# Output stores moved to ScalarE's DMA queue, and the U and V loads moved behind the last chunk of batch 0

## The chip, the core and the metric

The kernel runs on one core of one Trainium2 chip. The time is device microseconds (us) of one execution. The core has five engines that run side by side and wait for each other on semaphores: TensorE (PE in the profile, PEld for its weight loads), VectorE (DVE), ScalarE (ACT), GpSimd (POOL) and SyncE (SP). SyncE only starts DMAs here. In the traces below, VectorE, ScalarE and SyncE take their instructions in program order: a small copy on VectorE stands behind an addition that waits 18.8 us, although its own input is long ready. The granted clock is TensorE's clock as the chip granted it, as a share of full speed (1.00).

## The reference, cut to what matters

```python
# q, k, v: (4 batches, 8 heads, 768 positions, 64); out: (4, 768, 512), float32
for t in range(S):                                   # retention, per head
    state = gamma * state + outer(k[t], v[t])
    y[t] = scale * q[t] @ state
x = y as (B, 768, 512)
h = x.transpose(0, 2, 1) @ U @ V                     # U: 768x32, V: 32x768
u = x + h.transpose(0, 2, 1)
out = u + relu(u @ w_ch1) @ w_ch2                    # 512 -> 2048 -> 512
```

The kernel does the retention in 6 chunks of 128 positions per batch. It weaves the chunk work of batch b into the MLP of batch b-1.

## The kernel before

All inputs come through one list of loads, `feed`. SyncE issues the loads in that order into a ring of 28 buffers of 128x512 float32, and so runs up to 28 buffers ahead of GpSimd, which scales the inputs or casts them to bfloat16. U and V stand behind chunk 3 of batch 0 in the list.

```python
outp = ctx.enter_context(tc.tile_pool(name="outp", bufs=3))   # three output buffers
...
def feed_one():                         # the next load, on SyncE
    ...
    if key[0] == "uv":
        nc.sync.dma_start(out=Uf, in_=moe_U.rearrange("(j p) r -> p j r", p=P))
        for c in range(NCB):
            nc.sync.dma_start(out=Vf[ds(RK * c, RK)], in_=moe_V)
        return
    ...
    nc.sync.dma_start(out=t, in_=src)
...
for ci in range(NCK):
    feed_chunk(0, ci)
    if ci == 3:
        feed.append((("uv",), None))
# then w1 (16 tiles), batch 1's chunk 0, w2 (16 tiles), batch 1's chunk 1, ...
```

The last piece of each block of 128 output rows adds `u` and stores the result. The store is on SyncE too, behind every load that the program has issued up to then:

```python
def down(j, m0):                        # 4 of the 16 matmuls of output block j
    def f():
        ...
        if m0 == NM - 4:
            o_sb = outp.tile([P, DM], fp32, tag="o_sb", ...)
            nc.vector.tensor_tensor(o_sb, ch, us[b][:, j], op=ALU.add)
            nc.sync.dma_start(out=out[b, ts(j, P)], in_=o_sb)
    return f

def weave(pieces, *tracks):             # MLP pieces, other steps put between them
    ...
    for cost, f in pieces:
        while marks and marks[0][0] <= at:
            marks.pop(0)[1]()
        f()
        at += cost
...
weave(mlp_pieces(b - 1), (first, 0.03, 0.3),
      (steps, 0.42 if b == 1 else 0.15, 0.97))   # steps: chunks of batch b, then low rank
```

## Time and profile before

The time before is 270.7 us (median of 4 runs, 270.19 to 270.91). The profiled execution has a span of 267.2 us.

| stretch (us) | what TensorE does | PE busy | granted clock |
|---|---|---|---|
| 0 to 34.8 | batch 0's chunks, waiting for loads | 19.0 | 0.87 |
| 34.8 to 88.4 | batch 0's MLP, batch 1's chunks woven in | 50.9 of 53.6 | 0.96 (0.89 up to 56.7 us, then 1.00) |
| 88.4 to 102.9 | nothing | 0.2 of 14.5 | 0.58 |
| 102.9 to 111.7 | rest of the same stage | 8.2 of 8.8 | 0.72 |
| 111.7 to 220.8 | batches 1 and 2 | 107.4 of 109.1 | 1.00 |
| 220.8 to 267.2 | batch 3 | 42.4 of 46.4 | 1.00 |

From the page of the kernel before, the span in 40 slices of 6.7 us, counted from 1: busy tenths of TensorE, its granted clock in tenths, busy tenths of the DMA engines.

```profile
PE   1774689988999205999999999999999999999994
PEclk9996759999999755999999999999999999999999
DMA  8999998999999999697001021100001111000212
```

DMA is nearly full up to slice 19. TensorE is full from slice 7, but for a hole in slices 14 and 15, and the clock is low behind the hole. The waits view of the kernel before (engine, line, what was waited for, us, times, longest) names the two waits of the hole:

```profile
DVE o_3_1327 L335 <- DMA out_dram<-o_0_1089: 18.8, 1, 18.8
PE s_1372 L280 <- DVE pc_1366 L73: 14.3, 1, 14.3
```

Its timeline (start, us, engine, line, operation, output<-input, idle before and what ended it) gives the order of events on VectorE, SyncE and TensorE:

```profile
69.97 0.69 DVE L335 TENSOR_TENSOR o_0_1089<-mlp_1018,u_588 128x512 f32<-128x512 f32 x1 [2.32 <-PE mlp_1018 L330]
...
87.55 1.04 PE L330 MATMUL mlp_1332<-w2b,gT_685 128*128 128x512 bf16 x4
...
96.32 1.06 SPq L108 DMA_DIRECT2D in_1066<-in_q_dram  x1
97.47 1.07 SPq L336 DMA_DIRECT2D out_dram<-o_0_1089  x1
...
101.98 0.69 DVE L335 TENSOR_TENSOR o_3_1327<-mlp_1268,u_588 128x512 f32<-128x512 f32 x1 [18.83 <-DMA out_dram<-o_0_1089]
102.59 0.28 DVE L73 CAST pc_1366<-o_1341 128x128 bf16<-128x128 f32 x1
...
102.92 0.26 PE L280 MATMUL s_1372<-pc_1366,V_85 32*128 32x128 bf16 x1 [14.34 <-DVE pc_1366 L73]
...
111.69 1.03 PE L307 MATMUL mlp_1444<-uT_1331,w1b 128*128 128x512 bf16 x4
```

The addition o_0 was done at 70.66 us. SyncE issued its store at 97.47, 26.8 us later, behind further loads of about 1.1 us each. The fourth output block, o_3, needs o_0's buffer, so VectorE stood. The small copy of pc stands behind o_3 on VectorE, and TensorE needs pc. What the loads do to TensorE earlier shows at batch 1's chunk 1, again from the timeline of before:

```profile
57.24 1.04 POOL L174 TENSOR_TENSOR qd_1_916<-in_543,gq 128x512 bf16<-128x512 f32 x1 [0.67 <-DMA in_543<-in_q_dram]
58.52 0.38 PE L207 MATMUL qk_928<-ident,qd_1_916 128*128 128x128 bf16 x4
59.47 0.40 PE L209 MATMUL qk_928<-ident,kd_1_920 128*128 128x128 bf16 x4 [0.57 <-POOL kd_1_920 L174]
60.93 0.38 PE L217 MATMUL st_897<-vd_1_924,kd_1_920 128*128 128x128 bf16 x4 [1.06 <-POOL vd_1_924 L172]
```

GpSimd takes the chunk up as the loads land, and TensorE waits for GpSimd. At this point TensorE runs at the pace of the loads.

### The profile page before, as it was taken

What the parts mean: (1) busy time and instruction counts of PE and PEld (TensorE: products, weight loads), DVE (VectorE), ACT (ScalarE), POOL (GpSimd) and SP (SyncE); (2) the same over time, 40 slices, a digit from 0 to 9 for tenths busy, and PEclk for the clock granted to TensorE, in tenths of its full rate; (3) what the DMA queues carried; (4) which work ended last, traced back from release to release, by engine and by line L of the source; (5) the groups of instructions that cost most, each with busy time, mean ns of one, the idle gap of its engine ahead of it and who ended that gap; (6) DMA issues with size and microseconds to landing.
All of it is one profiled execution on the core that took longest, in us unless ns stands there. A gap on an engine that the chain in (4) does not pass through costs nothing.

```text
span 267.2 us, 4715 instructions
## 1 busy us (share of the span) xinstructions
PE 228.2 (85%) x1898; PEld 131.3 (49%) x1924; DVE 97.1 (36%) x178; ACT 95.1 (36%) x179; POOL 85.5 (32%) x113
## 2 busy tenths in 40 slices
PE   1774689988999205999999999999999999999994
PEld 1453524475555102445685545467855454475441
DVE  3330434523443004245554343455543425222211
ACT  2562334467442000346650203466611033552000
POOL 4766777877576700002333710030000000000000
PEclk9996759999999755999999999999999999999999
DMA  8999998999999999697001021100001111000212
GB/s 165 218 213 209 312 353 245 383 244 219 201 223 208 223 224 257 165 224 124 2 2 39 39 82 39 42 0 2 0 19 63 67 53 40 2 0 0 81 79 79
DMA packets 83942, 34.36 MB, mean 129 GB/s; under 512 B 76624, under 2 KB 76624, under 8 KB 83920
## 3 DMA queue, kind: packets, MB, share of 16 engines
q1 hardware_dynamic: 83920, 34.05, 55.0%
q8 instruction: 15, 0.25, 0.4%
q14 instruction: 7, 0.06, 0.1%
HBM read 27.75 MB, written 6.29 MB: 127 GB/s over the span
## 4 chain that ended last, share of the span: by engine, by line
PE 65%; DMA 19%; SPq 9%; POOL 2%; issue 2%; ACT 1%; DVE 1%; POOLq 0%; DVEq 0%
SPq L108 8%; DMA in_261<-in_q_dram 2%; DMA in_147<-in_moe_w_ch_dram 2%; DMA in_445<-in_moe_w_ch_dram 2%; DMA in_674<-in_q_dram 2%; DMA in_552<-in_q_dram 2%; DMA in_131<-in_moe_w_ch_dram 2%; DMA in_540<-in_moe_w_ch_dram 2%; DMA in_922<-in_v_dram 2%; DMA out_dram<-o_0_1089 2%; PE mlp_2807 L330 1%; PE mlp_2097 L330 1%; PE mlp_1183 L330 1%; PE mlp_2636 L330 1%; PE mlp_1988 L330 1%
## 5 line engine op out<-in xcount | busy, mean ns | idle before, releaser
L307 PEld LDWEIGHTS <-w1b 128*128 128x128 bf16 x512 | 48.2, 99 | 32.4 <-issue 3.0
L330 PEld LDWEIGHTS <-gT_2879 128*128 128x128 bf16 x96 | 9.4, 98 | 11.1
L280 PEld LDWEIGHTS <-V_85 32*128 32x128 bf16 x96 | 3.0, 98 | 21.9 <-issue 21.9
L330 PEld LDWEIGHTS <-gT_2169 128*128 128x128 bf16 x96 | 8.5, 98 | 8.9
L330 PEld LDWEIGHTS <-gT_1443 128*128 128x128 bf16 x96 | 8.5, 98 | 8.9
L280 PE MATMUL s_1372<-pc_1366,V_85 32*128 32x128 bf16 x4 | 0.6, 297 | 14.3 <-DVE pc_1366 L73 14.3
L330 PEld LDWEIGHTS <-gT_685 128*128 128x128 bf16 x96 | 8.4, 100 | 8.3 <-issue 1.5
L174 POOL TENSOR_TENSOR qd_5_1902<-in_926,gq 128x512 bf16<-128x512 f32 x1 | 1.0, 1042 | 25.9 <-PE qk_1520 L207 25.9
L71 ACT ACTIVATE uT_1331<-qk_1408 128x1024 bf16<-128x1024 bf16 x1 | 1.0, 1024 | 23.2 <-PE qk_1408 L292 23.2
L335 DVE TENSOR_TENSOR o_3_1327<-mlp_1268,u_588 128x512 f32<-128x512 f32 x1 | 0.7, 692 | 18.8 <-DMA out_dram<-o_0_1089 18.8
L174 POOL TENSOR_TENSOR qd_5_2612<-in_1554,gq 128x512 bf16<-128x512 f32 x1 | 1.0, 1042 | 19.9 <-PE qk_2240 L207 19.9
L207 PE MATMUL qk_194<-ident,qd_0_182 128*128 128x128 bf16 x4 | 0.6, 308 | 5.0 <-POOL qd_0_182 L174 5.0
L330 PE MATMUL mlp_1332<-w2b,gT_685 128*128 128x512 bf16 x15 | 4.8, 446 | 0.1
L330 PE MATMUL mlp_1403<-w2b,gT_685 128*128 128x512 bf16 x15 | 4.4, 430 | 0.3 <-issue 0.3
L330 PE MATMUL mlp_1183<-w2b,gT_685 128*128 128x512 bf16 x15 | 4.1, 381 | 0.1
L330 PE MATMUL mlp_1018<-w2b,gT_685 128*128 128x512 bf16 x15 | 4.1, 380 | 0.1
L330 PE MATMUL mlp_2636<-w2b,gT_2169 128*128 128x512 bf16 x15 | 3.9, 380 | 0.1
L330 PE MATMUL mlp_1875<-w2b,gT_1443 128*128 128x512 bf16 x15 | 3.9, 380 | 0.1
L330 PE MATMUL mlp_1926<-w2b,gT_1443 128*128 128x512 bf16 x15 | 3.9, 380 | 0.1
L330 PE MATMUL mlp_1268<-w2b,gT_685 128*128 128x512 bf16 x15 | 3.9, 380 | 0.1
L330 PE MATMUL mlp_2585<-w2b,gT_2169 128*128 128x512 bf16 x15 | 3.9, 380 | 0.1
L71 ACT ACTIVATE uT_2042<-qk_2129 128x1024 bf16<-128x1024 bf16 x1 | 1.0, 1023 | 8.2 <-PE qk_2129 L292 8.2
(980 smaller groups left out, 591.8 us busy)
## 6 DMA issues: line engine op xcount, KB each, us to landing
Vf<-in_moe_V_dram SPq DMA_DIRECT2D x4, 96.0 KB, 3.5
in_90<-in_q_dram SPq DMA_DIRECT2D x1, 256.0 KB, 3.0
in_92<-in_k_dram SPq DMA_DIRECT2D x1, 256.0 KB, 3.7
in_94<-in_v_dram SPq DMA_DIRECT2D x1, 256.0 KB, 4.3
in_96<-in_q_dram SPq DMA_DIRECT2D x1, 256.0 KB, 4.8
in_98<-in_k_dram SPq DMA_DIRECT2D x1, 256.0 KB, 5.0
in_100<-in_v_dram SPq DMA_DIRECT2D x1, 256.0 KB, 5.1
in_102<-in_q_dram SPq DMA_DIRECT2D x1, 256.0 KB, 5.1
```

The costliest lines, as they stand in the source:

```text
L71: nc.scalar.activation(dst, src, AF.Copy)
L108: nc.sync.dma_start(out=t, in_=src)
L174: nc.gpsimd.tensor_tensor(t, src, g[:, ci, :, None].to_broadcast([P, H, D]), op=ALU.mult)
L207: nc.tensor.transpose(tp[:, ts(p, P)], qd[:, ds(2 * p, 2)], ident)
L280: nc.tensor.matmul(banks[c - c0][:, ts(j - j0, P)], V4[ds(RK * c, RK), ts(j, P)], pcs[b][ds(RK * c, RK)], start=True, stop=True)
L307: nc.tensor.matmul(g_p[:, :sz], w1b[:, c, ts(m, P)], uTs[b][:, c, ds(lo, sz)], start=(c == 0), stop=(c == NCB - 1))
L330: nc.tensor.matmul(ch, gT[:, m, ts(j, P)], w2b[:, m], start=(m == 0), stop=(m == NM - 1))
L335: nc.vector.tensor_tensor(o_sb, ch, us[b][:, j], op=ALU.add)
```

## The change

There are two intents. Stores should not stand behind loads, so they go on ScalarE's queue, one MLP piece later, so that ScalarE does not wait for the addition. And batch 0's chunks 4 and 5 should not wait for U and V, which are needed only after chunk 5.

```diff
     for ci in range(NCK):
         feed_chunk(0, ci)
-        if ci == 3:
-            feed.append((("uv",), None))
+    feed.append((("uv",), None))
...
+    stores = []
+
+    def store():
+        if stores:
+            dst, src = stores.pop(0)
+            nc.scalar.dma_start(out=dst, in_=src)
...
-                    nc.sync.dma_start(out=out[b, ts(j, P)], in_=o_sb)
+                    stores.append((out[b, ts(j, P)], o_sb))
...
+            late = len(stores)
             f()
+            if late:
+                store()
             at += cost
         for _, f in marks:
             f()
+        while stores:
+            store()
...
             prep_chunk(0, ci + 1)
-            if ci + 1 == 3:
-                prep_uv()
+        else:
+            prep_uv()
```

## The prediction

> **What bounds the kernel now.** The slice view shows the DMA engines at 9 tenths for the first 97 us and TensorE at 9 tenths after 103. Between them is a hole. Timeline: the addition o_3 of batch 0 on VectorE waits 18.8 us (83.2 to 102.0) for the store of o_0, as there are three output buffers. That store was ready at 70.7, but SyncE reached it only at 97.5, behind some 25 input loads of about 1.1 us each (timeline of DMA issues). The copy of pc queues behind o_3, and TensorE idles from 88.4 to 102.9: 14.3 us in the waits view. The granted clock is then 0.50 to about 107.9 (2 us windows): four 128x512 matmuls take 1.82 us in place of 0.86.
>
> **The stores' move.** On ScalarE's queue the o_0 store issues near 71 us and lands about 4.4 later (its latency before), long before o_3 wants the buffer. The hole goes. From 88.4 to 111.7 TensorE took 23.3 us; the work in it at full clock is about 5.8 (24 matmuls of 0.216, 16 small expansions, 16 transposes), plus 0.5 of waits for the one transpose bank: 6.3. Gain about 17.0 us.
>
> Cost: 24 issues of 0.38 (free queue) to 1.1 us (full queue) on ScalarE, which is 36% busy and idles 0.7 to 2 us between instructions there; at most 0.3 us on the critical path. The Trainium skill ("DMA: Bandwidth & Descriptors", "Issuing engines are not separate DMA queues") says both queues share the 16 engines: six stores (1.5 MB) delay batch 2's loads by some 4 to 7 us at 220 to 380 GB/s. TensorE wants those only after 100 us; GpSimd had prepared most by 94. No loss. In batches 1 and 2, SyncE's waits of 23 and 32 us never held TensorE: each takes 54.5 us with TensorE busy 53.7.
>
> **The move of U and V.** Chunks 4 and 5 are prepared about 3.5 us earlier (U and V take 13.13 to 16.60 of SyncE's issue). The first MLP piece starts near 32 in place of 34.8, held by the first w1 casts (four done at 31.8). But the total of loads is the same and DMA is saturated: batch 1's chunk 1 still comes at 58.4 to 61, where TensorE already waits 1.9 us. The 3 us are paid back there. Worse, a gap near 3 us may drop the clock: the Trainium skill ("TensorE: Matmul & The Clock Gate", "Part 1: The HAM clock gate") says an idle window of about 3.4 us throttles to half; this trace agrees (the 2.84 us gap at 20 us and the 14.3 us one both led to 0.50, for about 5 us after work resumed). Between 0.5 us gained and 2.5 lost; I take 0.6 lost.
>
> **Prediction.** 270.66 - 17.0 + 0.6 = 254.3 us, range 251.8 to 257.0. Faster by over 2% 0.97, within 2% 0.025, slower 0.005.
>
> **What would show it.** Right: no wait of o_3 for the store; the 14.3 us wait for pc gone, clock 1.00 from 66 us on; stores on a second queue, landing in 3 to 6 us; the first MLP matmul near 32, but larger waits for batch 1's chunk 1 at 55 to 61; batches 1 and 2 still 54.5 us each, last batch 46.4. Wrong on U/V: that chunk arriving before 57.
>
> **What would make it wrong.** Stores starved by the loads' backlog, so that o_3 still waits; ScalarE's issue blocking so long that x and state evictions hold TensorE; stores slowing batch 1's chunk 5, which has 2.4 us of slack; a clock drop near 58 costing more than 2.5.

## The result

The changed kernel took 255.44 us (median of 4 runs, 254.50 to 256.59) against 270.7. The ratio is 0.9441, 95% interval 0.9391 to 0.9490, so it is faster, inside the predicted range of 251.8 to 257.0. A ratio here is the mean time of one kernel's fast runs over that of the other's of the same rounds, so it is not quite the ratio of the medians.

The same three rows from the page after (span 254.4 us, so slices of 6.4 us):

```profile
PE   0785789973999989999999999999999999999993
PEclk9997779996799999999999999999999999999999
DMA  8999899998999999999401111000012110000122
```

The hole at slices 14 and 15 is gone. There is a new, smaller one at slice 10, with a low clock behind it. Timeline after, at the old hole:

```profile
72.99 0.69 DVE L342 TENSOR_TENSOR o_0_1089<-mlp_1018,u_588 128x512 f32<-128x512 f32 x1 [2.31 <-PE mlp_1018 L337]
73.72 0.37 ACTq L303 DMA_DIRECT2D out_dram<-o_0_1089  x1
...
88.50 0.69 DVE L342 TENSOR_TENSOR o_3_1327<-mlp_1267,u_588 128x512 f32<-128x512 f32 x1 [2.33 <-PE mlp_1267 L337]
90.57 1.04 PE L337 MATMUL mlp_1331<-w2b,gT_685 128*128 128x512 bf16 x4
91.54 0.23 PE L279 MATMUL s_1372<-pc_1366,V_85 32*128 32x128 bf16 x1
...
98.92 1.03 PE L314 MATMUL mlp_1444<-uT_1330,w1b 128*128 128x512 bf16 x4
```

The o_0 store goes out 0.04 us after its addition ends (72.99 + 0.69) and lands 3.7 us later (list of DMA issues). The addition o_3 now waits for TensorE only, and TensorE meets pc without a wait. From the end of the four matmuls before pc is used to the next batch's first up-projection, TensorE took 23.3 us before (88.4 to 111.7) and 7.5 now (91.4 to 98.9): 15.8 us less. (The end of four matmuls is taken as 0.86 us after their start, since the next can start before the listed 1.04 us are over.)

At batch 1's chunk 1 the timeline after reads:

```profile
59.78 1.04 POOL L173 TENSOR_TENSOR qd_1_916<-in_543,gq 128x512 bf16<-128x512 f32 x1 [0.49 <-DMA in_543<-in_q_dram]
60.88 0.61 PE L206 MATMUL qk_928<-ident,qd_1_916 128*128 128x128 bf16 x4 [5.21 <-POOL qd_1_916 L173]
62.03 0.61 PE L208 MATMUL qk_928<-ident,kd_1_920 128*128 128x128 bf16 x4 [0.54 <-POOL kd_1_920 L173]
```

TensorE's MLP started at 32.7 us in place of 34.8, and TensorE reached this point about 3 us earlier than before. But the chunk came 2.5 us later than before. The gap of 5.2 us let the clock fall, as the 2 us windows after show (window, length, busy us of PE, PEld, DVE, ACT, POOL, granted clock, DMA share, GB/s):

```profile
58.00:60.00 2.00, 0.00 (x0) 0.00 (x0) 0.00 (x0) 0.00 (x0) 1.43 (x4) 0.95 0.52 114
60.00:62.00 2.00, 0.61 (x4) 0.35 (x4) 0.00 (x0) 0.00 (x0) 1.87 (x2) 0.50 0.93 207
62.00:64.00 2.00, 1.90 (x13) 1.47 (x14) 0.00 (x0) 1.26 (x2) 1.43 (x2) 0.50 1.01 214
```

So two questions were open. Is the whole gain the stores', and what about the late stores had cost the time? And does the U/V move bring anything, or does it cost, and through what?

### The profile page after: what moved, and what is told of

Its sections match the earlier page's. It is cut to its first block, busy times and chain, and to the rows that moved or that the text cites. A ratio compares the mean times of both kernels' runs of the same rounds, so it can differ in the third digit from the quotient of the medians.

```text
span 254.4 us, 4715 instructions
## 1 busy us (share of the span) xinstructions
PE 227.9 (90%) x1898; PEld 132.5 (52%) x1924; DVE 97.1 (38%) x178; ACT 95.0 (37%) x179; POOL 85.4 (34%) x113
## 4 chain that ended last, share of the span: by engine, by line
PE 71%; DMA 12%; SPq 10%; issue 2%; DVE 1%; ACT 1%; POOL 1%; POOLq 0%; DVEq 0%
SPq L108 9%; DMA in_543<-in_q_dram 3%; DMA in_257<-in_moe_w_ch_dram 3%; DMA in_145<-in_moe_w_ch_dram 3%; DMA in_491<-in_moe_w_ch_dram 2%; DMA in_321<-in_moe_w_ch_dram 2%; PE mlp_2096 L337 1%; PE mlp_2806 L337 1%; PE mlp_1182 L337 1%; PE mlp_2585 L337 1%; PE mlp_2697 L337 1%; PE mlp_1987 L337 1%; PE mlp_1925 L337 1%; PE mlp_2635 L337 1%; PE mlp_1018 L337 1%
## 5 line engine op out<-in xcount | busy, mean ns | idle before, releaser
L206 PE MATMUL qk_194<-ident,qd_0_182 128*128 128x128 bf16 x4 | 0.6, 305 | 5.3 <-POOL qd_0_182 L173 5.3
L206 PE MATMUL qk_928<-ident,qd_1_916 128*128 128x128 bf16 x4 | 0.6, 309 | 5.2 <-POOL qd_1_916 L173 5.2
L237 DVE TENSOR_TENSOR a_1_0_967<-s_957,mask 128x512 bf16<-128x512 f32 x1 | 0.7, 692 | 9.4 <-PE s_958 L233 9.4
L337 PE MATMUL mlp_1182<-w2b,gT_685 128*128 128x512 bf16 x15 | 4.1, 381 | 0.1
L337 PE MATMUL mlp_1018<-w2b,gT_685 128*128 128x512 bf16 x15 | 4.1, 380 | 0.1
L337 PE MATMUL mlp_1331<-w2b,gT_685 128*128 128x512 bf16 x15 | 3.9, 381 | 0.1
L337 PE MATMUL mlp_2585<-w2b,gT_2169 128*128 128x512 bf16 x15 | 3.9, 380 | 0.1
L337 PE MATMUL mlp_2635<-w2b,gT_2169 128*128 128x512 bf16 x15 | 3.9, 380 | 0.1
L337 PE MATMUL mlp_1925<-w2b,gT_1443 128*128 128x512 bf16 x15 | 3.9, 380 | 0.1
L337 PE MATMUL mlp_1267<-w2b,gT_685 128*128 128x512 bf16 x15 | 3.9, 380 | 0.1
L337 PE MATMUL mlp_1875<-w2b,gT_1443 128*128 128x512 bf16 x15 | 3.9, 380 | 0.1
L337 PE MATMUL mlp_1105<-w2b,gT_685 128*128 128x512 bf16 x15 | 3.7, 380 | 0.2 <-issue 0.2
```

Of the source, the lines that this page charges most:

```text
L206: nc.tensor.transpose(tp[:, ts(p, P)], qd[:, ds(2 * p, 2)], ident)
L237: nc.vector.tensor_tensor(a, four(sp[i]), causal(mask), op=ALU.mult)
L337: nc.tensor.matmul(ch, gT[:, m, ts(j, P)], w2b[:, m], start=(m == 0), stop=(m == NM - 1))
```

## The experiments

Theory A says: the gain comes from taking away VectorE's wait for a store; the U/V move costs time, as TensorE only arrives earlier at loads that come no earlier. Rivals are named with each run. "Changed kernel" means the kernel after. Each ratio is against the kernel before in the same rounds; the intervals are 95%. All twelve runs computed the right result.

### The changed kernel again, on the chip of the next three

No edit.

> The changed kernel once more, to have it on the chip of the three runs beside it and to see its two groups of times (254.5 to 254.7 at a granted clock of 0.98, 256.2 to 256.6 at 0.966). Expected 254 to 257 us. Theory A (the gap before batch 1's chunk 1 sometimes costs the full clock and sometimes not): slow and fast times of this kernel again differ by the clock, about 2 us for 0.013 of clock. Rival: the times scatter at one clock.

Measured: 255.08 us median of 5 (254.25 to 255.14), ratio 0.9449 (0.9423 to 0.9476). The part on the clock failed: a run at a mean clock of 0.965 took 255.14 us, one at 0.980 took 255.08. Mean granted clock and time do not go together here.

### The stores' move alone

```diff
-    feed.append((("uv",), None))          # and prep_uv behind chunk 5
+        if ci == 3:
+            feed.append((("uv",), None))  # and prep_uv behind chunk 3, as before
```

> The stores' move alone; U and V stay behind chunk 3. Theory A (the whole gain is the stores', and the U/V move costs time, because it only makes TensorE arrive earlier at batch 1's chunk 1, whose loads come no earlier): 252 to 254 us, 1 to 3 us below the changed kernel; before chunk 1 TensorE waits 1.9 us in three waits as before, and the clock stays 1.00 from 42 us on. Rival B (the U/V move brings its 3 us and the stores' move less than 17): 256 to 258.5 us, above the changed kernel.

Measured: 253.44 us median of 4 (253.09 to 253.84), ratio 0.9396 (0.9370 to 0.9422). The mean is 253.46 against 254.92 of the changed kernel on the same chip, and no run of the one reaches a run of the other. The stores' move gains 16.3 us (269.76 - 253.46), and the U/V move on top costs 1.5. The clock is 1.00 from 42 us on and the waits before chunk 1 are the old ones, 0.34 and 0.97 us. Rival B falls.

### The U/V move alone

```diff
-        if ci == 3:
-            feed.append((("uv",), None))
+    feed.append((("uv",), None))          # prep_uv behind chunk 5; stores on SyncE
```

> The U/V move alone; stores stay on SyncE as before. Theory A: 270 to 273 us, no faster than before: a gap of 3 to 5 us before batch 1's chunk 1, and the hole at o_3 still ends when SyncE reaches the o_0 store at about 97.5 us or up to 2 us later. Rival B: about 267.5 us.

Measured: 269.77 us median of 6 (269.25 to 271.62), ratio 1.0009 (0.9979 to 1.0039). The gap before chunk 1 is 4.3 us. The old hole stays, 14.0 us of waiting for pc, and swallows the loss: it ends when SyncE reaches the o_0 store, at 98.07 us. The move brings nothing alone.

### Six output buffers, nothing else

```diff
-    outp = ctx.enter_context(tc.tile_pool(name="outp", bufs=3))
+    outp = ctx.enter_context(tc.tile_pool(name="outp", bufs=6))
```

> The kernel before with six output buffers in place of three, and nothing else: the stores stay on SyncE behind the loads, U and V stay. It tells what about the late store cost the time. Theory A (only the wait of o_3, o_4, o_5 for a buffer stops VectorE, then TensorE): the hole goes although the o_0 store still goes out near 97 us; 252 to 254.5 us, like the stores' move alone. Rival C (the stores on SyncE's queue cost time also by holding back the loads, or the second queue is needed for bandwidth): the time stays above 257 us.

Measured: 253.67 us median of 5 (253.13 to 254.23), ratio 0.9403 (0.9378 to 0.9428): the same as the stores' move alone. Its timeline shows that the o_0 store is as late as ever and o_3 no longer cares:

```profile
85.89 0.69 DVE L335 TENSOR_TENSOR o<-mlp,u 128x512 f32<-128x512 f32 x1 [2.33 <-PE mlp L330]
...
97.96 1.90 SPq L336 DMA_DIRECT2D out_dram<-o  x1
```

So the late store itself cost nothing, nor did SyncE's queue need relief. The whole cost was the reuse of the buffer. A second queue and three more buffers (6 KB in each partition) are two cures of one wait. Rival C falls.

### Stores later, but still on SyncE

```diff
-            nc.scalar.dma_start(out=dst, in_=src)     # in the stores' move alone
+            nc.sync.dma_start(out=dst, in_=src)
```

> The kernel before with the stores one MLP piece later but still on SyncE's queue. Theory A: nothing is gained, 269 to 271 us; the o_0 store still goes out at 97 to 98 us behind the loads and TensorE still waits 14 us for pc. If the delay alone mattered: clearly below 268 us.

Measured: 270.40 us median of 4 (269.32 to 270.84), ratio 0.9994 (0.9964 to 1.0024). The waits view has the same two waits:

```profile
DVE o L343 <- DMA out_dram<-o: 20.4, 2, 19.2
PE s L280 <- DVE pc L73: 14.8, 1, 14.8
```

The delay alone is worth nothing.

### Stores on ScalarE, but at once

```diff
-            late = len(stores)
             f()
-            if late:
+            while stores:
                 store()
```

> The changed kernel, but each store issued on ScalarE's queue right behind its addition, not one MLP piece later. Theory A: the delay is not what brings the gain; within 0.5 us of the changed kernel (254.5 to 256). If the delay matters, ScalarE would wait in order for VectorE's addition and hold up evictions that TensorE needs: over 256.5 us.

Measured: 256.12 us median of 4 (256.05 to 257.39), ratio 0.9489 (0.9463 to 0.9516), a little above the expected band and about 1 us above the changed kernel, whose interval it just touches. The profile shows where such a loss can sit, once in each of batches 1 and 2. The transposes of u that wait for ScalarE's eviction of uT, with the store and the eviction before them in this run, then with the eviction in the changed kernel's second profile:

```profile
147.72 0.34 ACTq L303 DMA_DIRECT2D out_dram<-o  x1
148.10 1.02 ACT L71 ACTIVATE uT<-qk 128x1024 bf16<-128x1024 bf16 x1 [8.19 <-DVE o L342]
149.18 0.61 PE L291 MATMUL qk<-ident,u 128*128 128x128 bf16 x8 [0.91 <-ACT uT L71]
```

```profile
147.79 1.02 ACT L71 ACTIVATE uT<-qk 128x1024 bf16<-128x1024 bf16 x1 [8.18 <-PE qk L291]
148.86 0.61 PE L291 MATMUL qk<-ident,u 128*128 128x128 bf16 x8 [0.25 <-ACT uT L71]
```

ScalarE stands at the store, waiting for VectorE's addition, while the eviction behind it is ready to go: TensorE waits 0.66 us longer, twice. These two waits make 1.3 us, which my expectation had taken for nearly nothing. The measured times agree in size, but with intervals that overlap they do not settle it alone.

### The gap filled with useless matmuls

```diff
+                    if (b, i) == (1, 1):
+                        w = bank("s")
+                        for _ in range(20):
+                            nc.tensor.matmul(w, w1b[:, 0, :P], w1b[:, 0, :512],
+                                             start=True, stop=True)
                     turn(b, i, "A" if b == 1 else "D")
```

> The changed kernel with 20 useless 128x512 matmuls (about 4.3 us at full clock) put before the transposes of batch 1's chunk 1, where TensorE waits 3.1 to 5.2 us for the loads; their result is overwritten. It separates the gap itself from the clock drop behind it. Theory A (the gap also costs clock): granted clock stays 1.00 from 42 us on, and the time is 0.4 to 1.2 us below the changed kernel's, 254.0 to 254.7. Rival D (the clock drop is free, since TensorE only waits for chunk 2 afterwards): the same time or up to 1 us more, as the filler overruns the gap.

Measured: 255.16 us median of 5 (254.54 to 256.18), ratio 0.9444 (0.9419 to 0.9469), the changed kernel's time. It missed its aim: the clock fell all the same, only later, as the windows show.

```profile
60.00:62.00 2.00, 0.58 (x8) 0.41 (x8) 0.00 (x0) 0.00 (x0) 1.83 (x3) 1.00 0.96 211
62.00:64.00 2.00, 1.72 (x15) 1.28 (x13) 0.00 (x0) 1.67 (x3) 1.44 (x2) 0.71 1.19 224
64.00:66.00 2.00, 2.00 (x16) 1.11 (x15) 0.92 (x2) 0.77 (x2) 1.70 (x3) 0.50 1.26 226
```

Between the filler and the next real work TensorE waited 1.1, 0.7 and 0.3 us with short transposes between, and right behind them the clock fell. That these waits were the cause is the reading that the next run tests.

### The gap and the short waits filled

```diff
+        warm(1, 1, 24)     # before the transposes of chunk 1
...                         # q transposes
+        warm(b, ci, 3)     # then the k transposes
+        warm(b, ci, 2)     # then the state matmuls (chunk 1 of batch 1 only)
```

> The first filler run missed its aim: the granted clock still fell to 0.50 at about 63 us, as the short waits behind the filled gap left TensorE mostly idle. Here 24 useless 128x512 matmuls stand before the transposes of batch 1's chunk 1, 3 more between its q and its k transposes, and 2 behind them. Theory A: the clock is 1.00 from 42 to 100 us; chunk 2's state matmuls then start within 0.3 us of the end of its v copy on GpSimd (0.7 to 1.2 us late in the changed kernel's profiles), and the time is 0.4 to 1.2 us below the changed kernel's, 253.8 to 254.7 us. Rival D (the drop costs nothing): 255 us or more.

Measured: 254.84 us median of 6 (254.29 to 255.66), ratio 0.9432 (0.9399 to 0.9465). This time the clock was 1.00 from 42 us on, and the state matmuls of chunk 2 started right behind GpSimd's copy of its v:

```profile
64.72 0.61 POOL L171 CAST vd<-in 128x512 bf16<-128x512 f32 x1
65.38 0.38 PE L226 MATMUL st<-vd,kd 128*128 128x128 bf16 x4 [0.31 <-POOL vd L171]
```

In the changed kernel's first profile that copy ended at 66.2 us and the matmuls started at 67.3, so the cold clock delayed TensorE by about 1.2 us there. But the time is not clearly below the changed kernel's: by the ratios it is 0.5 us below, and the intervals overlap. These runs do not resolve what the clock drop costs. With the clock kept, the run is still about 1.0 us above the stores' move alone by the ratios (0.9432 against 0.9396; means 254.94 and 253.46 us, in other rounds and on another chip). These intervals overlap too, and the filler may cost a little itself, so how the 1.5 us divide between the clock and the later loads is not shown.

### Batch 1's chunks woven in later

```diff
-              (steps, 0.42 if b == 1 else 0.15, 0.97))
+              (steps, 0.56 if b == 1 else 0.15, 0.97))
```

> The changed kernel with batch 1's chunk work woven in from 0.56 of batch 0's MLP on, not from 0.42: all up-projections and some down-projections first. It tests whether the 3 us of the U/V move come out once TensorE does not run into batch 1's loads. Theory A: the 3 to 5 us gap before chunk 1 shrinks below 1.5 us, the clock stays at 1.00 behind it, and the time falls to 249.5 to 252.5 us, under the stores' move alone (253.4). Rival (what is lost sits elsewhere, or the denser weave costs as much as the gap): 254 us or more.

Measured: 251.93 us median of 6 (250.67 to 252.66), ratio 0.9315 (0.9289 to 0.9342). This beats both kernels; its interval lies clear of the changed kernel's (0.9423 to 0.9476) and of the stores' move alone (0.9370 to 0.9422). TensorE reaches chunk 1 when it is there, and the waits for loads shrink to two short ones. What is left to gain is at the end of the stage, where the crowded low-rank steps wait for VectorE:

```profile
65.11 0.38 PE L216 MATMUL st<-vd,kd 128*128 128x128 bf16 x4 [0.37 <-POOL vd L171]
69.04 0.38 PE L216 MATMUL st<-vd,kd 128*128 128x128 bf16 x4 [0.71 <-POOL vd L171]
87.58 0.38 PE L279 MATMUL s<-pc,V 32*128 32x128 bf16 x7 [0.39 <-DVE u L283]
88.71 0.23 PE L291 MATMUL qk<-ident,u 128*128 128x128 bf16 x1 [0.53 <-DVE u L283]
89.31 0.56 PE L291 MATMUL qk<-ident,u 128*128 128x128 bf16 x5 [0.36 <-DVE u L283]
```

### The later weave, with U and V back behind chunk 3

```diff
-    feed.append((("uv",), None))          # on top of the later weave
+        if ci == 3:
+            feed.append((("uv",), None))
```

> The later weave start of 0.56 with U and V back behind chunk 3: what the U/V move is worth once the gap is out of the way. Theory A (the move gives TensorE 2 to 3 us more before batch 1's loads, kept only if the work there does not wait for them): 1 to 2.5 us above the later start with U/V moved (251.9), so 253 to 254.5, no better than the stores' move alone. Rival (the move is worth nothing or less, the later start alone did it): 251 to 252.3 us.

Measured: 252.33 us median of 6 (251.49 to 254.45), ratio 0.9352 (0.9312 to 0.9393). That is 1.0 us above the later weave by the ratios, below the band that theory A gave, and the intervals overlap. From 50 us on, its profile shows no wait of TensorE for a load at all, so the later weave closes the gap with U and V in either place. Whether the U/V move is worth anything once the gap is gone stays open; if it is, it is about 1 us and not 2 to 3.

### A weave start in between

```diff
-              (steps, 0.42 if b == 1 else 0.15, 0.97))
+              (steps, 0.50 if b == 1 else 0.15, 0.97))
```

> The changed kernel with the weave start at 0.50, between 0.42 and 0.56. With 0.56 the last low-rank steps of batch 1 are crowded and TensorE waits 1.5 us for VectorE at 87 to 90 us; with 0.42 it waits 4 us for chunk 1's loads. Theory A: a gap of 1 to 2.5 us before chunk 1, less waiting at the end; 250.8 to 253 us, about as good as 0.56. A time over 254 us would say that the gap's length does not set the loss.

Measured: 253.38 us median of 6 (251.99 to 254.51), ratio 0.9378 (0.9341 to 0.9416), 0.4 us over the expected band. It lies between 0.42 and 0.56, as the length of the waits before chunk 1 does: 1.7 us in three waits here. The longest of them, 0.95 us, ended with ScalarE's eviction of chunk 0's transposes and not with a load, so this run does not cleanly test the gap's length.

### U and V on ScalarE's queue

```diff
+    def load_uv():                        # the same five loads
+        nc.scalar.dma_start(out=Uf, ...)
+        for c in range(NCB):
+            nc.scalar.dma_start(out=Vf[ds(RK * c, RK)], in_=moe_V)
...
         turn(0, ci, "A")
+        if ci == 3:
+            load_uv()
```

> The changed kernel with the five U and V loads taken off SyncE's queue: ScalarE issues them after its evictions of batch 0's chunk 3, at about 18 us, so they share the DMA engines with chunks 4 and 5 and w1 follows chunk 5 directly on SyncE's queue. With U and V behind the last chunk the DMA engines were less busy from 22 to 32 us (share 0.82 to 0.86, 214 to 234 GB/s) than with them behind chunk 3 (0.92 to 0.97, 243 to 258 GB/s), and batch 1's chunk 1 came 1 to 2.5 us later. Theory E (what slows the stream is the small loads standing alone at the change from the chunks to w1, not their lateness): share 0.92 or more from 22 to 32 us, chunk 1's q copied on GpSimd before 58.0 us, and a time of 252.5 to 254.5 us. Rival (the number of bytes alone sets when chunk 1 comes, and the difference was chance): 58.3 us or later, and 254.5 to 256 us.

Measured: 256.24 us median of 6 (254.07 to 257.54), ratio 0.9498 (0.9451 to 0.9545), DMA share 0.88 from 22 to 32 us, and chunk 1 taken up at 60.05 us. Theory E missed on every count. But the run is no clean test of it either, as it added a wait of its own, in SyncE's waits between 18 and 36 us:

```profile
SPq L102 <- DMA Uf<-in_moe_U_dram: 5.6, 1, 5.6
```

By the releaser that the profile infers, SyncE held chunk 5's v load until ScalarE's U load had landed at 24.8 us. So why the stream of loads is slower with U and V behind the last chunk stays open. That it is slower shows without exception in the profiles, one of each run. With U and V behind chunk 3 there are five: before, the stores' move alone, six buffers, stores later on SyncE, and the later weave with U and V back. In these GpSimd took up chunk 1's q at 57.2 to 57.9 us, and from 22 to 32 us the loads moved 243 to 263 GB/s. In the other eight, all with U and V behind the last chunk on SyncE's queue, it was 58.3 to 59.8 us and 214 to 241 GB/s.

## Why the prediction was right

The time, 255.44 us, lies in the range, 1.1 us above the 254.3 predicted. The two sizes that were off, 0.7 us in the stores' gain and 0.9 us in the U/V move's loss, add up and do not cancel, so the hit does not come from two errors that hide each other. Point by point:

- **The hole and its cause: right.** VectorE's wait for o_0's store and TensorE's for pc are gone, and six buffers do the same as a second queue. The waits are the cause, not the queue.
- **"Gain about 17.0 us": somewhat too large.** The stores' move alone measured 16.3 us. The term at fault is the 6.3 us that I put for the work left between 88.4 and 111.7 us; it took 7.5. The text counts 24 matmuls where the trace has 20, so the big matmuls were not short-counted; what was too small are the waits (0.32, 0.16, 0.28 and 0.25 us make 1.0, not 0.5) and the transposes and small expansions between them.
- **Cost on ScalarE: right.** The issues took 0.34 to 0.40 us, and TensorE shows no wait for them. They come one piece later; issued at once, they go with 0.66 us more of TensorE waiting in each of batches 1 and 2.
- **"No loss" from delayed loads of batch 2: right, with some luck in the size.** GpSimd finished its v copy of chunk 4 of batch 2 at 97.9 us in place of 93.9, the low end of the 4 to 7 us, and TensorE began that batch's first chunk later still. But the second profile of the same kernel has 96.2 us and the stores' move alone 96.4, so what the stores delay is nearer 2.5 us, below the range.
- **Batches 1 and 2 unchanged: right.** They start 54.5 us apart after (98.92, 153.37 and 207.83 us).
- **The U/V move paid back and worse: right in sign, mis-sized.** "I take 0.6 lost" measured 1.5. "Batch 1's chunk 1 still comes at 58.4 to 61" is the step that failed: TensorE could start on it at 60.9 us in the first profile after and 59.6 in the second, with loads 1 to 2.5 us later. I had looked for the loss in the clock. The clock did drop, but in the run with the clock kept up about 1.0 us of loss remained; that the later loads are the larger part is likely and not shown.
- **"Clock 1.00 from 66 us on": nearly.** It was 0.85 from 66 to 68 us, then 1.00.

On the skill: the prediction leaned on two pages. The Trainium skill, "DMA: Bandwidth & Descriptors", section "Issuing engines are not separate DMA queues", says that DMAs of all engines run on the same 16 DMA engines and interleave, and that another issuing engine "will only save the time on the sequencer". The traces fit the shared engines (with the stores' move alone, batch 2's loads fell behind by 2.5 us). What the store saved was sequencer time too, but not that of one DMA: it had stood 26.8 us behind the issues of 21 loads that SyncE had before it in order. The Trainium skill, "TensorE: Matmul & The Clock Gate", section "Part 1: The HAM clock gate (the "warmup" mystery)", gives half clock after an idle window of about 3.4 us and full clock after a busy one. The traces agree in kind: 0.50 behind the gaps of 14.3 and 5.2 us, and no drop in the run that filled the gap and the short waits behind it.

## What to carry to other kernels

When a result waits for an old output buffer, ask where the old store stands in its queue, not how fast DMA is: a store behind a deep prefetch waits for all of it, and either a queue of its own or enough buffers cures that equally. A store issued by a computing engine should come in program order after something that makes its data ready for sure, or the engine stands with it. And an earlier start of one stage brought nothing here while the next ran at the pace of the loads; what helped was to put work first that had its data, as the later weave did (0.9315 against 0.9449 of the time before).

## What the Trainium skill lacked or had wrong

- "DMA: Bandwidth & Descriptors" has nothing on a store waiting in program order behind prefetched loads on the same issuing queue: the store was ready at 70.7 us and issued at 97.5, and its removal from that queue gained 16.3 us. The sequencer time that another engine saves is there, but not that a store can stand behind the issues of many loads, nor that more buffers cure that as well (253.7 us with six buffers, 253.4 with the other queue).
- The same page gives no issue time on a full queue. One 256 KB load of q, k or v held SyncE's queue about 1.1 us while the DMA engines were saturated; a store on ScalarE's queue in the same stretch took 0.34 to 0.40 us to issue and 3.6 to 5.6 us to land.
- "TensorE: Matmul & The Clock Gate" gives no measure of how much waiting, mixed with short matmuls and transposes, counts as an idle window: behind about 3 us with waits of 1.1, 0.7 and 0.3 us the clock dropped in the first filler run, while behind a similar stretch in the kernel before (waits of 0.6 and 1.1 us at 58.5 to 61 us) it did not.
- No page says what order of small and large loads keeps the DMA engines full: five loads of 96 KB at the change from chunks to w1 went with 214 to 241 GB/s over 10 us, the same five between chunks with 243 to 263. The cause was not found here.
